# Channel products by seven block products, with weights and weight sums streamed from DRAM

## The chip, the cores and the metric

The kernel runs on one core of a Trainium2 chip. The metric is device time in microseconds of one execution; lower is better. Before the change three executions took 1118.13, 1116.75 and 1111.63 us, median 1116.75.

## The reference

Attention with a causal mask and a decay, then a token mixer and a channel mixer:

```python
batch, n_heads, seq, head_dim = (8, 8, 576, 64)      # B, H, S, D
scores = scale * q @ k.T                             # per head
decay = cum[:, None] - cum[None, :]                  # cum = cumsum(log f)
attn = softmax(where(causal, -1e9, scores + decay))
x = (attn @ v)                                       # (8, 576, 512)
xt = x.transpose(0, 2, 1)
h = np.maximum(xt @ w_tok1, 0.0) @ w_tok2            # tokens: 576 -> 256 -> 576
u = x + h.transpose(0, 2, 1)
h2 = np.maximum(u @ w_ch1, 0.0) @ w_ch2              # channels: 512 -> 1536 -> 512
return (u + h2).astype(np.float32)
```

B x S gives N = 4608 tokens. The channel mixer is the part that changes: per token two products with a 512 x 1536 and a 1536 x 512 matrix.

## The kernel before

**Precision.** A float32 product is made of three matmuls of a rounded type: each operand is split in a high part (ACT, `hi_act`, L575) and a low part, value minus high (`lo_dve` L584, on POOL `lo_pool` L581; behind a relu `lo_relu` L587), and high x high, low x high and high x low are summed in PSUM. So every product of a 128 x 128 weight block with up to 512 columns of tokens is three matmuls.

**Weights** come in as pairs of 32-bit words and are decoded by `decode` (L650): a raw tile `d_raw` of 128 x 512 pairs is loaded, some six steps on ACT and DVE (two tensor_scalars at L675 and L679, then L683, L687, L691) make float32 values in `d_g`, and ACT and DVE write their high and low parts. A piece of 512 columns is called a unit here.

**Stages.** First attention, head by head, with the token mixer of one batch entry laid between the heads of the next. `mixer` (L1193) transposes the attention output, makes the two token products (`tok1` L1252, `tok2` L1276) and, in the same pass, the first F1 = 2 of the NF = 12 hidden blocks of 128 of the channel mixer (`ch1` L1321, `ch2` L1349). It spills u (`ud`) and the partial channel sums (`pd`) to DRAM.

Then comes the channel stage with the remaining F2 = 10 hidden blocks, over nine chunks of 512 tokens. Its 20 weight units (10 of the first matrix, `w1r`, 10 of the second, `w2r`) stay in SBUF, in pools that `swap` (L1488) opens where attention's buffers were. `rest` (L743) decodes them; the first six run during the last mixer pass and the others early in the channel stage. `begin` (L1084) loads a chunk's u (into `xt`) and partial sums (into `part`), splits u into eight `ring` tiles and adds u to the partial sums on POOL. `up` (L1118) makes one hidden block: 12 matmuls of 512 columns (L1135 to L1137), relu and split (ACT L575, DVE L587) into `hid`. `down` (L1145) multiplies it into four PSUM accumulators by another 12 matmuls (L1156 to L1158); after the last block DVE adds the partial sums (L1169) and SP stores the result (L1173). The loop at L1177 runs `up` one block ahead of `down`.

**Order.** All instructions are registered with `Plan` (L362), a list scheduler that takes each with a priority, a cost and its buffers, and emits one fixed order per engine at build time. The priority counts blocks of the channel stage from `base`. SP issues all loads and stores in that order; a row that waits holds back what stands behind it.

Of the kernel before, what the change touches and what calls it, by code (L numbers as in the profile page):

```python
# [356 lines left out]

class Op:
# [3 lines left out]
class Plan:  # L362
# [9 lines left out]
    FIFO = ("ring", "xt", "part", "pr", "hl", "k1", "k2", "vv", "raw", "vr", "p34", "p2", "p1", "p0", "low", "hid", "d_raw", "d_g", "qf", "f34", "f2", "f1", "f0")  # L372
# [161 lines left out]
def build(nc, env, dims):  # L534
# [59 lines left out]
    cc = Buf("cc")  # L594

# [3 lines left out]
    def decay():  # L599
# [9 lines left out]
        p.op("POOL", 600, pr, lambda: nc.gpsimd.memset(row(2), 0.0), wr=["zero"], bufs=[w])  # L609
# [40 lines left out]
    def decode(prio, loads, w, hi, lo, tok, late=None):  # L650
        rb, gb = Buf("d_raw"), Buf("d_g")
# [6 lines left out]
        for i, (rows, cols, src) in enumerate(loads):  # L658
            dma(prio - 1.0, lambda a=(rows, cols, src): ld(*a), nb / len(loads), wr=[(rb, i)], bufs=[rb])
        rd = [(rb, i) for i in range(len(loads))]  # L660
# [38 lines left out]
        p.op("DVE", d_dve(w), prio, s6, port=True, rd=rd, wr=[gb], bufs=[rb, gb])  # L699
        p.op("ACT", d_act(w, False), prio, lambda: hi_act(hi(), asf(tl()[2])), rd=[gb, *([late] if late else [])], wr=[(tok, "h")], bufs=[gb])  # L700
# [3 lines left out]
        )  # L704

# [5 lines left out]
    def dec_list():  # L711
# [31 lines left out]
        def rest(i, which):  # L743
            def go(prio):
                if which == 1:
                    fs = sl((F1 + i) * P, P)
                    loads = [(full, sl(c * P, P), w_ch1[sl(c * P, P), fs]) for c in range(NC)]
                else:
                    loads = [(full, sl(0, C), w_ch2[sl((F1 + i) * P, P), :])]
                key = f"w{which}r"  # L750
# [5 lines left out]
            return go  # L756
# [3 lines left out]
        third = [rest(i, w) for i in range(F2) for w in (1, 2)]  # L760
# [296 lines left out]
    DB = PRM["DB"] if F1 else 0  # L1057
    whole = [(x * HS, HS, True) for x in range(2 * DB)]
    rest_, n_ch = N - DB * S, -(-(N - DB * S) // 512)
    cuts = [DB * S + x * rest_ // n_ch for x in range(n_ch + 1)]  # L1060
# [477 lines left out]
```

## Time and profile before

| what | before |
|---|---|
| three executions | 1111.63 to 1118.13 us, median 1116.75 |
| span of the profiled execution | 1116.7 us |
| granted TensorE clock in it, mean | 0.983 |
| PE busy | 1076.1 us |
| DVE, ACT, POOL busy | 633.4, 557.8, 536.7 us |
| moved by DMA | 148.43 MB |
| channel stage, first matmul start to last | 619.96 to 1111.82 us |

How to read the rows that follow below: PE is the matrix engine, PEld its weight loads, DVE, ACT and POOL the vector, scalar and general engines, SP the engine that issues DMAs. In a grouped row stand the source line, engine, operation, output <- inputs and a count, then busy time and mean nanoseconds of one, then idle time of the engine just before them and what ended it. In a timeline row the first number is the start and the second the duration; what stands in brackets is the idle time before it with its releaser. Durations overlap: two operations in a row can start closer together than one lasts, so the distance of starts, the pace, is what a busy engine spends on one.

### The profile page before, as it was taken

How to read it: one execution, taken by the hardware profiler on the slowest of the kernel's cores; microseconds unless marked ns; L12 is line 12 of the kernel's file. 1: busy time of each engine (PE TensorE's matmuls, PEld its weight loads, DVE VectorE, ACT ScalarE, POOL GpSimd, SP SyncE). 2: the span in 40 equal slices, each digit the busy share in tenths (PEclk: the TensorE clock that was granted, in tenths of full speed). 3: DMA queues.
4: the chain of work that ended last, by engine and by line, in shares of the span. 5: the costliest groups of instructions: out<-in, count | busy, mean ns of one | idle time of the engine just before them, and what ended most of it. 6: DMA issues, size and time to landing. Idle time of an engine off the chain costs nothing.

```text
span 1116.7 us, 18738 instructions
## 1 busy us (share of the span) xinstructions
PE 1076.1 (96%) x6442; PEld 939.2 (84%) x6442; DVE 633.4 (57%) x1618; ACT 557.8 (50%) x1441; POOL 536.7 (48%) x615
## 2 busy tenths in 40 slices
PE   8896988999999999999999999999999999999998
PEld 5565877899999999999998888888888888888886
DVE  5778989787887878888788992121212121111111
ACT  4675866788887888887885542111111111111110
POOL 4577797787868877787852205030312121111010
PEclk8898999999999999999999999999999999999999
DMA  8686587878768778687643635130303030302011
GB/s 198 157 202 149 153 214 179 209 197 201 208 168 209 201 193 218 168 214 192 168 132 131 183 102 175 36 114 1 113 1 113 1 113 0 114 19 57 24 53 38
DMA packets 70831, 148.43 MB, mean 133 GB/s; under 512 B 10008, under 2 KB 27416, under 8 KB 69712
## 3 DMA queue, kind: packets, MB, share of 16 engines
q1 hardware_dynamic: 70608, 147.22, 49.3%
q8 instruction: 51, 0.84, 0.3%
q14 instruction: 44, 0.36, 0.1%
q10 hardware_dynamic: 128, 0.01, 0.0%
HBM read 63.46 MB, written 28.31 MB: 82 GB/s over the span
## 4 chain that ended last, share of the span: by engine, by line
PE 77%; DVE 7%; DMA 7%; POOL 3%; ACT 2%; SPq 2%; issue 1%; DVEq 0%; POOLq 0%; ACTq 0%
PE bank L1135 7%; PE bank L1136 7%; PE bank L1137 7%; PE pair L1156 7%; PE pair L1158 7%; PE pair L1157 7%; PE bank L917 6%; DMA k<-hl 6%; PE bank L861 5%; PE pair L861 2%; PE pair L997 2%; PE pair L999 2%; PE bank L1276 1%; PE bank L1278 1%; PE pair L987 1%
## 5 line engine op out<-in xcount | busy, mean ns | idle before, releaser
L587 DVE SCALAR_TENSOR_TENSOR hid<-bank,hid 128x512 fp32r<-128x512 f32 x90 | 62.2, 691 | 337.1 <-ACT hid L575 336.9
L581 POOL TENSOR_TENSOR ring<-xt,ring 128x512 fp32r<-128x512 f32 (+1 forms) x68 | 92.3, 1372 | 315.4 <-ACT ring L575 314.6
L575 ACT ACTIVATE hid<-bank 128x512 fp32r<-128x512 f32 x90 | 53.8, 598 | 344.2 <-PE bank L1137 344.2
L903 POOL TENSOR_SCALAR pr<-pr,rec 128x576 f32<-128x576 f32 (+4 forms) x320 | 172.4, 558 | 38.4 <-DVE rec L896 31.0
L575 ACT ACTIVATE p<-bank 128x384 fp32r<-128x384 f32 (+2 forms) x300 | 128.5, 476 | 41.3 <-PE bank L917 38.9
L917 PE MATMUL bank<-ident,pr 128*128 128x128 f32 (+1 forms) x960 | 141.0, 282 | 7.9 <-DVE p L584 5.6
L1136 PE MATMUL bank<-ring,w1r 128*128 128x512 f32 x360 | 140.1, 389 | 0.0
L1135 PE MATMUL bank<-ring,w1r 128*128 128x512 f32 x360 | 140.1, 389 | 0.0
L1158 PE MATMUL pair<-hid,w2r 128*128 128x512 f32 x360 | 140.1, 389 | 0.0
L1157 PE MATMUL pair<-hid,w2r 128*128 128x512 f32 x360 | 140.1, 389 | 0.0
L1156 PE MATMUL pair<-hid,w2r 128*128 128x512 f32 x360 | 140.0, 389 | 0.0
L1137 PE MATMUL bank<-ring,w1r 128*128 128x512 f32 x360 | 140.0, 389 | 0.0
L875 ACT ACTIVATE pr<-bank,nmin 128x448 f32<-128x448 f32 (+3 forms) x256 | 118.3, 469 | 26.0 <-DVE nmin L868 23.8
L917 PEld LDWEIGHTS bank<-ident,pr 128*128 128x128 f32 (+1 forms) x960 | 110.6, 134 | 20.1 <-DVE p L584 6.1
L584 DVE TENSOR_TENSOR p<-bank,p 128x384 fp32r<-128x384 f32 (+1 forms) x180 | 106.1, 594 | 27.5 <-ACT p L575 26.4
L868 DVE CUSTOM_DVE_ANT_0 bank<-bank,mask 64x64 f32<-64x64 f32 (+3 forms) x256 | 106.7, 433 | 14.5 <-PE bank L861 12.7
L861 PE MATMUL bank<-k 128*128 128x320 f32 (+1 forms) x496 | 89.3, 301 | 9.4 <-DMA k<-hl 5.8
L861 PEld LDWEIGHTS bank<-k 128*128 128x128 f32 x496 | 75.6, 179 | 22.5 <-DMA k<-hl 5.5
L1158 PEld LDWEIGHTS pair<-hid,w2r 128*128 128x128 f32 x360 | 67.6, 188 | 14.2
L1137 PEld LDWEIGHTS bank<-ring,w1r 128*128 128x128 f32 x360 | 67.6, 188 | 14.1
L1156 PEld LDWEIGHTS pair<-hid,w2r 128*128 128x128 f32 x360 | 67.6, 188 | 14.0
L1136 PEld LDWEIGHTS bank<-ring,w1r 128*128 128x128 f32 x360 | 67.6, 188 | 14.0
(125 smaller groups left out, 2451.7 us busy)
## 6 DMA issues: line engine op xcount, KB each, us to landing
k<-hl SPq DMA_DIRECT2D x186, 288.0 KB
raw<-in_qk SPq DMA_DIRECT2D x31, 576.0 KB
vr<-in_v SPq DMA_DIRECT2D x32, 320.0 KB
ud<-xt SPq DMA_DIRECT2D x8, 1152.0 KB
pd<-part SPq DMA_DIRECT2D x32, 288.0 KB
out_t<-part SPq DMA_DIRECT2D x36, 256.0 KB
d_raw<-in_w_ch SPq DMA_DIRECT2D x12, 512.0 KB
d_raw<-in_w_ch SPq DMA_DIRECT2D x40, 128.0 KB
```

The source lines that it names most:

```text
L575: nc.scalar.activation(out, in_, func, scale=scale)
L861: nc.tensor.matmul(ps[:m, of : of + w], k[:, 0, i0 : i0 + m], k[:, 1, j0 : j0 + w], start=(x == 0), stop=(fq or x == 1))
L868: nc.vector.tensor_tensor_reduce(x, x, E["mask"][:m, a : a + w], -1.0 / D**0.5, 3e38, op0=ALU.add, op1=ALU.min, accum_out=E["nmin"][sm][:m ...
L875: nc.scalar.activation(at(pr)[:m, poff[t] : poff[t] + w], at(buf)[:m, of : of + w], AF.Exp, bias=E["nmin"][sm][:m, t : t + 1], scale=-1.0, ...
L903: nc.gpsimd.tensor_scalar(x, x, r, 0.0, op0=ALU.mult, op1=ALU.add)
L917: nc.tensor.transpose(out, at(pr)[:, poff[i] + start[j] : poff[i] + end[j]], E["ident"])
L1135: nc.tensor.matmul(q, wh[:, c, :], h_, start=(c == 0), stop=False)
L1136: nc.tensor.matmul(q, wl[:, c, :], h_, start=False, stop=False)
L1137: nc.tensor.matmul(q, wh[:, c, :], l_, start=False, stop=(c == NC - 1))
L1156: nc.tensor.matmul(q, wh, h_, start=(i == i0), stop=False)
L1157: nc.tensor.matmul(q, wl, h_, start=False, stop=False)
L1158: nc.tensor.matmul(q, wh, l_, start=False, stop=(i == NF - 1))
```

## The change

The channel stage is written anew. Three things change.

**768 tokens directly.** Two chunks, of 512 and 256 tokens (`PLAIN`), go through the ten hidden blocks as before, but block by block together: per block 12 matmuls of 512 and 12 of 256 up (`plain_up`, L1219 to L1221), and as many down (`plain_down`, L1239 to L1241). Meanwhile the weights are decoded. At the end DVE adds the partial sums (L1246) and SP stores (L1250).

**3840 tokens by seven products.** They form four super chunks of 2 x 480 tokens. Both channel products are done as a 2 x 2 block product by Strassen's scheme in Winograd's form, with seven block products in place of eight; the blocks are halves of the tokens and halves of the matrices. `prep` (L1301) makes the sums of u that the scheme needs and splits them. The up half goes over five pairs q of hidden blocks: per pair seven `uprod` of 6 matmuls with 480 columns (L1365 to L1367), the results combined from PSUM by ACT and DVE into four float tiles `H` (`plus` L1287, and L1390, L1396, L1402). The down half goes over the seven products: `product` (L1409) splits an operand made of `H` tiles into a `st` or `hid` tile for each pair and multiplies it (`mul`, 6 matmuls, L1440 to L1442); `diff` (L1277) makes the next operands out of the `H` tiles on DVE; `join` and `leave` (L1472, L1480) combine the results with partial sums and u, which `rest_in` (L1450) loads and POOL adds, and store them. So a super has 5 x 7 x 6 matmuls up and as many down. The first 42 up matmuls of the next super are laid between the last 42 down ones of this one.

**Weights through DRAM.** `unit` (L721) takes the place of `rest`. A unit is now four blocks of 128 x 128. Beside the split that it had (`pw` tile), DVE makes four sums of its blocks (128 columns each), these are split too (`sg` tile), and both are stored to DRAM (`wd`), 393 KB and 524 KB. In the supers one 256 KB tile of them is loaded per product (`weights`, L1296) into twelve half tiles. In exchange SBUF no longer holds all the weights; the raw, ring and token weight tiles are used again for other purposes, and a third `swap` opens `H` and `st` tiles after the direct stage.

The core of the diff:

```diff
-        def rest(i, which):
-                decode(
-                    prio, loads, C, lambda: E[key][i][:, 0, :], lambda: E[key][i][:, 1, :], (key, i),
-                    late=f"gate{int(i >= PAIRS0)}",
-                )
+    def unit(prio, loads, which, q, k, gate_, i):
+        gb = decode(prio, loads, C, None, None, i, late=gate_)
+        pb, sb = Buf("pw"), Buf("sg" if i < 8 else "sg2")
...
+        for out, a, b, op in ((0, (0, 3), (0, 2), ALU.add), (1, (1, 0), (0, 0), ALU.subtract), (3, (0, 1), (1, 1), ALU.subtract), (2, (0, 0), (0, 3), ALU.subtract)):
+            p.op(
+                "DVE", d_dve(P), prio + SLAG / UNIT,
+                lambda out=out, a=a, b=b, op=op: nc.vector.tensor_tensor(blk(1, out), blk(*a), blk(*b), op=op),
...
+        for x, (b, z0, z1) in enumerate(((pb, 0, 3), (sb, 3, 7))):
+            dma(
+                prio, lambda b=b, z0=z0, z1=z1: nc.sync.dma_start(E["w_d"][which][q][:, z0:z1, k], asf(at(b)[:, : z1 - z0])), P * 1024 * (z1 - z0), rate=340,
...
-    base = HB + 20
+    base = HB + 220
...
+    for i in range(F2):
+        clock = i * tile_us
+        for ch in chunks:
+            plain_up(i, ch)
+        if i:
+            clock = (i - 1) * tile_us
+            for ch in chunks:
+                plain_down(i - 1, ch)
...
+    def weights(which, q, z):
+        wq = Buf("wq")
+        dma(
+            pr(14), lambda: nc.sync.dma_start(asf(at(wq)), E["w_d"][which][q][:, z]), P * 2048,
...
+        def uprod(q, z, bank, first, fin, extra=(), more=()):
+            wq = weights(1, q, z)
+            bs = [ub[z, k] for k in (0, 1)]
...
+                for k in (0, 1):
+                    wt, h_, l_ = at(wq)[:, k], at(bs[k][0])[:, :w], at(bs[k][1])[:, :w]
+                    nc.tensor.matmul(o, wt[:, 0, :], h_, start=(first and k == 0), stop=False, skip_group_check=True)
+                    nc.tensor.matmul(o, wt[:, 1, :], h_, start=False, stop=False, skip_group_check=True)
+                    nc.tensor.matmul(o, wt[:, 0, :], l_, start=False, stop=(fin and k == 1), skip_group_check=True)
...
+        def product(z, src, bank, first, relu, fin=False, lead=9.0):
...
+            for x in range(FX):
+                st, hb = Buf("st"), H[x][src]
...
+                dve(
+                    lead, lambda st=st, hb=hb: (lo_relu if relu else lo_dve)(at(st)[:, 1, :w], at(hb)[:, :w], at(st)[:, 0, :w]),
...
+        product(0, 0, "a", True, False, lead=25.0)
...
+        for x in range(FX):
+            diff(b12[x], b12[x], b11[x], 18.0 - 1.3 * x, True)
+        product(3, 1, "c", True, False)
...
+        product(2, 2, "d", False, False, fin=last)
+        leave(1, 0, "d", 2 if last else 1)
```

Everything up to the last mixer pass keeps its order on every engine. Three places of the order differ in ways that matter below.

The first is DVE in that last mixer pass (the batch entry's `ring` tiles are the hidden tokens of the token product, which PE waits for; `d_g`, `tmp` are weights in decoding). Before:

```order
L584 TENSOR_TENSOR ring_138<-bank_67,ring_135 128x512
L584 TENSOR_TENSOR ring_140<-bank_65,ring_139 128x512
L584 TENSOR_TENSOR ring_141<-bank_68,ring_141 64x256
L1290 TENSOR_TENSOR xt_130<-bank_66,xt_130 128x288
L1290 TENSOR_TENSOR xt_130<-bank_67,xt_130 128x288
L584 TENSOR_TENSOR w1r_6911<-d_g_146,w1r_6911 128x512
L675 TENSOR_SCALAR d_g_147<-d_g_147 128x512
L587 SCALAR_TENSOR_TENSOR ring_137<-bank_65,ring_136 128x512
```

After:

```order
L593 TENSOR_TENSOR ring_149<-bank_67,ring_149 64x256
L593 TENSOR_TENSOR pw_6918<-d_g_156,pw_6918 128x4x128
L690 TENSOR_SCALAR d_g_157<-d_g_157 128x512
L686 TENSOR_SCALAR tmp_6921<-tmp_6921 128x512
L694 SCALAR_TENSOR_TENSOR d_g_157<-d_raw_155,d_g_157 128x512
L690 TENSOR_SCALAR tmp_7244<-tmp_6921 128x512
L698 TENSOR_TENSOR d_g_157<-d_g_157 128x512
L694 SCALAR_TENSOR_TENSOR tmp_7244<-d_raw_154,tmp_7244 128x512
L702 SCALAR_TENSOR_TENSOR d_g_157<-d_raw_155,d_g_157 128x512
L596 SCALAR_TENSOR_TENSOR ring_151<-bank_65,ring_150 128x512
```

Ahead of the relu of the hidden tokens (the last row of each) now stand steps of two units in decoding.

The second is SP where the supers begin. Before, in the channel stage, it only fetched chunks and stored results:

```order
L1093 DMA xt_130<-ud_110 128x4x320
L1173 DMA out_t<-part_151 128x512
L1173 DMA out_t<-part_150 128x512
L1096 DMA part_151<-pd_116 128x128
L1096 DMA part_151<-pd_117 128x384
```

After:

```order
L1250 DMA out_t<-d_raw_153 128x256 x2
L1250 DMA out_t<-d_raw_154 128x256
L1296 DMA pw_6915<-wd_1_124 128x512
L1250 DMA out_t<-d_raw_154 128x256
L1296 DMA pw_6915<-wd_1_124 128x512
L1296 DMA pw_6916<-wd_1_124 128x512
L1296 DMA pw_6918<-wd_1_124 128x512
L1296 DMA pw_6916<-wd_1_124 128x512
L1296 DMA pw_6918<-wd_1_124 128x512
L1458 DMA d_raw_153<-pd_116 128x384
```

Weight tiles of the supers (`pw<-wd`) now stand between and behind the stores of the direct tokens, and the loads of partial sums and u behind them.

The third is DVE in the channel stage. Before, one relu a block and four adds a chunk:

```order
L587 SCALAR_TENSOR_TENSOR hid_6913<-bank_65,hid_6913 128x512
L1169 TENSOR_TENSOR part_148<-pair_63,part_148 128x512
L587 SCALAR_TENSOR_TENSOR hid_6913<-bank_66,hid_6913 128x512
L1169 TENSOR_TENSOR part_150<-pair_63,part_150 128x512
L1169 TENSOR_TENSOR part_149<-pair_64,part_149 128x512
```

After, in the down half of a super:

```order
L1402 TENSOR_TENSOR h_8389<-bank_65,tmp_8393 128x480
L1334 TENSOR_TENSOR xt_140<-xt_140 128x480
L593 TENSOR_TENSOR hid_6922<-h_8376,hid_6922 128x480
L593 TENSOR_TENSOR hid_6923<-h_8380,hid_6923 128x480
L1281 SCALAR_TENSOR_TENSOR h_8376<-h_8375,h_8376 128x480
L1281 SCALAR_TENSOR_TENSOR h_8380<-h_8379,h_8380 128x480
L593 TENSOR_TENSOR hid_6924<-h_8384,hid_6924 128x480
L593 TENSOR_TENSOR w2l<-xt_140,w2h 128x480
```

Low parts of operands (L593), differences of `H` tiles (L1281) and sums of the next super's u (L1334) alternate, where relus stood alone.

More of the change, by code (lines that the diff above doesn't have):

```diff
@@ L371 @@
     START = dict(PE=3000, DVE=900, ACT=1900, POOL=1810, SP=700)
-    FIFO = ("ring", "xt", "part", "pr", "hl", "k1", "k2", "vv", "raw", "vr", "p34", "p2", "p1", "p0", "low", "hid", "d_raw", "d_g", "qf", "f34", "f2", "f1", "f0")
+    FIFO = ("ring", "xt", "part", "pr", "hl", "k1", "k2", "vv", "raw", "vr", "p34", "p2", "p1", "p0", "low", "hid", "hidB", "pw", "sg", "sg2", "uh", "uh2", "H", "st", "wq", "q", "rr", "g2", "d_raw", "d_g", "qf", "f34", "f2", "f1", "f0")
     def __init__(self):
@@ L650, in decode @@
     def decode(prio, loads, w, hi, lo, tok, late=None):
-        rb, gb = Buf("d_raw"), Buf("d_g")
+        rb, gb = Buf("d_raw"), Buf("g2" if late and tok > 1 else "d_g")
         nb = P * w * 8
@@ new lines, in build, with pr, weight, tile_of @@
+    FX = F2 // 2
+    W = (N - sum(PLAIN)) // 8
+    clock = 0.0
+    def pr(lead=0.0):
+        return base + (clock - lead) / UNIT
+    def weight(which, i, c):
+        k, m = (c, i % 2) if which == 1 else (i % 2, c)
+        unit_ = pw[which, i // 2, (c % 2)]
+        half, row = (c // 2, i % 2) if which == 1 else (i % 2, c // 2)
+        return unit_, (0, 3, 1, 2)[2 * half + row]
+    def tile_of(which, i, c):
+        b, x = weight(which, i, c)
+        return at(b)[:, x, 0, :], at(b)[:, x, 1, :]
@@ new lines, in build, with dve, diff, f @@
+    gate("gate2", [q for q in p.ops if any(z.kind in ("pw", "g2") for z in q.bufs)], lambda: E["swap"](2))
+    w = W
+    mm1 = w / 2.4e3 + 0.013
+    clock = tile_us * F2
+    NSC = (N - T1) // (2 * w)
+    last = False
+    def dve(lead, fn, **k):
+        return p.op("DVE", d_dve(w), pr(lead), fn, **k)
+    def diff(out, a, b, lead, relu=False):
+        def f():
+            o_, a_, b_ = (at(x)[0][:, at(x)[1], :w] if isinstance(at(x), tuple) else at(x)[:, :w] for x in (out, a, b))
+            if relu:
+                nc.vector.scalar_tensor_tensor(o_, a_, 0.0, b_, op0=ALU.max, op1=ALU.subtract)
+            else:
+                nc.vector.tensor_tensor(o_, a_, b_, op=ALU.subtract)
+        dve(lead, f, rd=[a, b], wr=[out], bufs=list({a, b, out}), port=True)
@@ L1444, in attn_mixer_kernel @@
     E["part_d"] = [dram.tile([P, NC, S], F32, name=f"pd{b}") for b in range(B)]
+    E["w_d"] = {which: [dram.tile([P, 7, 2, 2, P], F32, name=f"wd{which}_{q}") for q in range(F2 // 2)] for which in (1, 2)}
+    E["q"] = E["acc"] | E["one"]
+    E["two"] = E["accB"] = E["one"]
+    E["sg"], E["uh"] = {}, {}
+    for nm in ("t1h", "t1l", "t2h", "t2l", "w1h", "w1l", "w2h", "w2l"):
+        x = E[nm].rearrange("p a b -> p (a b)")
+        if nm[:2] == "t1":
+            E["sg"][((nm, 0), (nm, 1))] = x[:, : 2 * C].rearrange("p (z h n) -> p z h n", z=4, h=2)
+        for i in (0, 1):
+            E["uh"][((nm, i),)] = x[:, i * C : (i + 1) * C]
+    E["sg2"], E["uh2"] = E["sg"], E["uh"]
     for _ in range(3):
```

533 lines of the change are left out of this document (415 added, 118 removed).

## The prediction

> **What bounds the kernel now.** I read the page's totals first, then the forty slices, the chain, and last the windows and single rows of the channel stage, where the change lies.
>
> ```profile
> PE 1076.1 (96%) x6442; PEld 939.2 (84%) x6442; DVE 633.4 (57%) x1618; ACT 557.8 (50%) x1441; POOL 536.7 (48%) x615
> PE   8896988999999999999999999999999999999998
> DVE  5778989787887878888788992121212121111111
> PE 77%; DVE 7%; DMA 7%; POOL 3%; ACT 2%; SPq 2%; issue 1%; DVEq 0%; POOLq 0%; ACTq 0%
> L587 DVE SCALAR_TENSOR_TENSOR hid<-bank,hid 128x512 fp32r<-128x512 f32 x90 | 62.2, 691 | 337.1 <-ACT hid L575 336.9
> L1158 PEld LDWEIGHTS pair<-hid,w2r 128*128 128x128 f32 x360 | 67.6, 188 | 14.2
> ```
>
> PE is busy 96% of 1116.7 us. The slices show two regimes: up to about slice 23 DVE is nearly as full as PE; from there, the channel stage, DVE falls to 1 or 2 tenths while PE stays at 9. The only DVE work there, 90 relus, idles 337 us waiting on ACT, which waits on PE. So in this stage the matmul count times the period of one matmul is the time, and DVE and DMA are nearly free. The windows say how free (columns: us, then busy time and count of PE, weight loads, DVE, ACT, POOL, then clock, DMA share, GB/s):
>
> ```profile
> 0.00:560.00 560.00, 525.89 (x3822) 475.65 (x3823) 454.25 (x1305) 427.04 (x1192) 423.04 (x518) 0.97 0.75 190
> 620.00:640.00 20.00, 20.00 (x90) 16.53 (x90) 19.67 (x35) 9.24 (x16) 1.29 (x1) 1.00 0.61 193
> 641.00:642.00 1.00, 1.00 (x7) 0.80 (x6) 0.97 (x3) 0.73 (x2) 0.00 (x0) 1.00 0.80 256
> 649.00:650.00 1.00, 1.00 (x6) 0.83 (x5) 1.00 (x4) 0.20 (x1) 0.00 (x0) 1.00 0.88 263
> 685.00:687.00 2.00, 2.00 (x10) 1.68 (x9) 0.28 (x1) 0.00 (x0) 0.60 (x1) 1.00 1.04 322
> 688.00:690.00 2.00, 2.00 (x11) 1.65 (x10) 0.57 (x1) 0.93 (x2) 0.21 (x1) 1.00 1.06 377
> 700.00:800.00 100.00, 100.00 (x443) 82.81 (x442) 17.73 (x27) 15.16 (x26) 20.49 (x16) 1.00 0.19 57
> ```
>
> From 700 to 800 us PE is busy throughout at full clock, DVE 18%, DMA 57 GB/s.
>
> **Part 1, the matmuls.** Periods come from starts on PE's timeline.
>
> ```profile
> 619.96 0.40 PE L1135 MATMUL bank<-ring,w1r 128*128 128x512 f32 x1
> 1101.16 0.39 PE L1156 MATMUL pair<-hid,w2r 128*128 128x512 f32 x1
> 1106.60 0.39 PE L1156 MATMUL pair<-hid,w2r 128*128 128x512 f32 x1
> 601.28 0.28 PE L1252 MATMUL bank<-ring,t1h 128*128 128x256 f32 x1
> 604.51 0.28 PE L1253 MATMUL bank<-ring,t1l 128*128 128x256 f32 x1
> 606.71 0.29 PE L1276 MATMUL bank<-t2h,ring 128*128 128x288 f32 x1
> 608.31 0.29 PE L1276 MATMUL bank<-t2h,ring 128*128 128x288 f32 x1
> 1111.82 0.39 PE L1158 MATMUL pair<-hid,w2r 128*128 128x512 f32 x1
> ```
>
> The two starts 5.44 us apart in the second and third row are 24 matmuls (one block up, one down): 0.2267 us each at 512 columns. The 256-column pair is 27 intervals in 3.23 us: 0.1196. The difference is 0.000418 us a column, and 288 columns come to 0.133 by it: 12 intervals in 1.60 us agree. So 480 columns should take 0.2133. Before: 9 chunks x 10 blocks x 24 = 2160 matmuls of 512, 489.7 us (619.96 to 1111.82 is 491.9, of which 2.4 are the last 18 matmuls of the mixer's second channel product, which only move ahead of the stage in the new order: no net cost). After: 240 of 512 (54.4) and 240 of 256 (28.7) direct, then 4 supers x (210 up + 210 down) = 1680 of 480 (358.3): 441.4. The term is 441.4 - 489.7 = **-48.3 us**. It is a gain only if everything that the seven products need keeps up with a PE that is already full; the other parts price that.
>
> **Part 2, DVE ahead of the direct stage.** DVE's durations and paces:
>
> ```profile
> 631.90 0.42 DVE L675 TENSOR_SCALAR d_g<-d_g 128x512 uint32<-128x512 uint32 x1
> 632.23 0.68 DVE L587 SCALAR_TENSOR_TENSOR hid<-bank,hid 128x512 fp32r<-128x512 f32 x1
> 632.84 0.68 DVE L584 TENSOR_TENSOR w2r<-d_g,w2r 128x512 fp32r<-128x512 f32 x1
> 633.43 0.42 DVE L679 TENSOR_SCALAR d_g<-d_g 128x512 uint32<-128x512 uint32 x1
> 633.89 0.69 DVE L683 SCALAR_TENSOR_TENSOR d_g<-d_raw,d_g 128x512 f32<-128x512 uint32 x1
> 586.33 0.55 DVE L584 TENSOR_TENSOR p<-bank,p 128x384 fp32r<-128x384 f32 x1
> 587.86 0.20 DVE L584 TENSOR_TENSOR low<-bank,p 64x64 fp32r<-64x64 f32 x1
> 605.46 0.69 DVE L587 SCALAR_TENSOR_TENSOR ring<-bank,ring 128x512 fp32r<-128x512 f32 x1 [2.29 <-ACT ring L575]
> 606.21 0.40 PE L1276 MATMUL bank<-t2h,ring 128*128 128x288 f32 x1 [1.41 <-DVE ring L587]
> ```
>
> Start to start, a 512-column op takes 0.605 us and a tensor_scalar 0.335 (0.455 where it needs the op just ahead of it, 633.43 to 633.89). 0.55 against 0.68 for 384 and 512 columns is 0.0011 a column, so 480 columns are 0.571 and 128 about 0.20. In the last mixer pass PE waits 1.41 us on one DVE relu, and DVE had idled 2.29 just before it. In the new order DVE has six 512-column ops, four tensor_scalars and one 128-column op more in that stretch (weights are decoded two and three units at a time): 3.6 + 1.3 + 0.2 = 5.2 us. What idled and what ran slow there, 2.8 us, absorbs the rest: **+2.4**, between 0 (if DVE takes these after the relu in effect, by running ahead) and +5.2.
>
> **Part 3, the direct stage.** One block now lasts 12 x 2 x (0.2267 + 0.1196) = 8.31 us of PE, and two weight units are decoded in it. From block 3 to block 9 DVE has 9 decodes, 10 sets of four 128-column sums with their low parts, 13 relus and 5 ops of 480: 50.5 us by the paces above, against 6 x 8.31 = 49.9 of PE. With all 18 tensor_scalars at the dependent price it is 52.7: **+2.8**. That is a dead heat, as the window 620 to 640 (DVE 19.67 of 20) shows DVE can be: bounds 0 and +12.7 (each op at its duration, 0.69, not at its pace). DMA: a unit loads 0.52 MB and stores 0.92 MB, 1.44 MB in about 5.5 us = 262 GB/s; the loads of the same raw weights in 1 KB runs reach 256 to 263 GB/s at shares of 0.80 to 0.88, about 305 at a full share. It fits, with little to spare; the stores stand on the same queue, SP's, ahead of the next raw loads, so a late low part holds back the loads behind it, and the three raw buffers are what hides that.
>
> **Part 4, into the supers.** The first super's splits of u and the second hidden pair's weights come late: on SP those weights stand behind the stores of the direct tokens, which wait for their adds. The first six products have their buffers filled ahead, 1.28 us of PE each. I take **+1.5**, between 0 and +4 (three products late).
>
> **Part 5, the supers.** A super is 420 x 0.2133 = 89.6 us of PE. DVE has about 120 ops of 480, 68.4 us, so on average it is covered; it was 18 us in 100. But the ops are not even: a hidden pair of the up half has 7 or 8 (4.0 to 4.6 us in 8.96), the down half 84 (48.0 us in 44.8), since each product's operand is built, rounded high and low per pair. The next super's first 42 up matmuls are laid between the last 42 down ones, so the down half lasts nearer 52. Six operand buffers let DVE run six steps (7.7 us) ahead. I take +1 a super, **+4** in all, bounds 0 and +40. POOL adds eight sums a super beside it, all due in the light half; what POOL does to DVE:
>
> ```profile
> 610.34 1.56 DVE L691 SCALAR_TENSOR_TENSOR d_g<-d_raw,d_g 128x512 uint32<-128x512 uint32 x1
> 611.82 1.93 DVE L687 TENSOR_TENSOR d_g<-d_g 128x512 f32<-128x512 f32 x1
> ```
>
> Beside POOL two such ops took 1.56 and 1.93 us, not 0.69: about 1 us lost each, 8 us a super, inside the 21 us that DVE has free; without that cover they would cost it in full.
>
> DMA in a super: 70 tiles of 256 KB of weights (18.4 MB), u twice, partial sums and the output (7.9 MB): 26.2 MB in 89.6 us = 292 GB/s, five times what the stage moves now. The rows 685 to 690 (u and partial sums in 2 KB runs) reach 322 and 377 at a share of 1.04 to 1.06. The new tiles have 2 KB runs too. SP takes its instructions in order, so the weights also stand behind stores that wait for DVE's adds; twelve tiles, 15 us of products, hide that. I take no wait from it, and keep the other end for rival C. How such loads are issued:
>
> ```profile
> 685.75 4.72 SPq L1096 DMA_DIRECT2D part<-pd  x6
> 1110.95 2.65 DVE L1169 TENSOR_TENSOR part<-pair,part 128x512 f32<-128x512 f32 x4 [2.83 <-PE pair L1158]
> 1111.67 2.29 SPq L1173 DMA_DIRECT2D out_t<-part  x4
> ```
>
> SP spends 4.72 / 6 = 0.79 us on an issue; some 90 issues a super are 71 us of 89.6. The Trainium skill, "DMA: Bandwidth & Descriptors", section "Anatomy of one DMA", gives about 2.0 us fixed plus bytes at 436 GB/s for one transfer (measured on GpSimd's path), and its "Bandwidth" section asks for 1 MiB or more; an estimate by it is 2.6 us for a 256 KB tile, 182 us a super if they came one after another, and so speaks against this change. The trace does not agree with "one after another": 322 GB/s over 2 us is 2.5 tiles landed in 2 us, so several overlap. By the page the sum would end near 1450; loading in that fashion is the far end of rival C.
>
> **Part 6, the end.** The last matmul starts at 1111.82 and the span ends at 1116.7, with four adds of 512 and four stores behind it. The new end adds two halves of 240 columns, two stores: **-0.8** (0 to -1.5).
>
> **The sum**, against the profiled execution, whose span of 1116.7 is also the median of the three runs (1116.75): 1116.7 - 48.3 + 2.4 + 2.8 + 1.5 + 4.0 - 0.8 = **1078.3 us**. Call it case A. Its own range is 1066 to 1092: the lower end has every addition at nothing (1066.8), the upper the direct stage and the supers some 7 each beyond what I took.
>
> **Rivals.**
>
> B, DVE sets the pace of the down halves. If its 480-column ops cost their duration (0.55 + 96 x 0.0011 = 0.66) and not their pace, 84 are 55.4 us against 44.8 of PE. Half the operand buffers' lead (3.8) pays for some: 6.8 a super, 27 in place of 4: 1101. For it: DVE at 19.67 of 20 us in the decode window shows no reserve to draw on, and every operand passes ACT first. Against: there 512-column ops held their pace of 0.605.
>
> C, the other side: the weight stream sets the pace of the supers. Loads and stores mixed ran, over the first 560 us, 190 GB/s at a share of 0.75: 253 at a full share. At that rate a super's 26.2 MB take 103.6 us, 14.0 over PE, 56 for four in place of 4: 1130. It decides from 261 GB/s downward: there a super takes 100.2 us, and the 42.4 us of four such delays eat the gain. Fewer than three tiles in flight would do the same: the stores at the end need about 3 us each (the last is issued near 1113.5, the end is 1116.7), so two in flight give 175 GB/s, three 262. Against: 256 KB transfers in 2 KB runs reached 322 and 377, and the program has twelve tiles to fill.
>
> D, the matmuls don't get shorter: a 480-column matmul keeps 0.2267, because the weight load ahead of it (188 ns, the row above) and its switch set the period. 1680 x 0.0134 = 22.5: 1100.8. Against: 288 and 256 columns scale, at 0.133 and 0.1196, with the same weight loads.
>
> **How the numbers follow.** A has a chance of 0.70, B 0.14, C 0.10, D 0.06. The forecast is A's 1078.3. The range reaches from 1065 to 1103, so that it takes in B's and D's times; outside are C and the outer parts of the others, about 0.2. One per cent, 11.2 us, is about what can be told from no change here. Faster than 1105.6 are A, B, D and a fifth of C: 0.92. Within 1%: 0.03, from C near its break-even; slower than 1127.9: 0.05, the other half of C.
>
> **What would show it.** Right: the matmul starts of the supers 0.2133 apart, PE busy 9 tenths or more throughout, DMA near 290 GB/s in the supers and DVE near 0.75; direct stage 83 to 90 us, a super 89.6 to 92. B would show as PE idle before L1440 released by DVE on st or hid tiles, C as PE idle before L1365 or L1440 released by DMA on pw tiles, D as a 0.227 period. The prediction is wrong if supers take over 96 us, or if the time before the direct stage grows by more than 5.

## The result and the profile after

The changed kernel takes 1087.28 us (median of four runs, 1086.0 to 1093.99), the kernel before 1116.05 (median of four as well). The ratio is 0.9759, interval 0.9725 to 0.9794: faster by 2.4%. The forecast was 1078.3 us, with a range of 1065 to 1103. The profiled execution took 1088.3 us with a span of 1086.1, 30.6 less than the 1116.7 that the prediction started from.

The page of the changed kernel: totals, the slices of PE, DVE and DMA, and the chain.

```profile
PE 1037.6 (96%) x6442; PEld 921.1 (85%) x6442; DVE 887.8 (82%) x2114; ACT 646.9 (60%) x1607; POOL 496.6 (46%) x579
PE   8897888999999999999999899999999999999998
DVE  5778989787787888878879999975995896797486
DMA  8686577686877868777675799789999889979874
PE 69%; DVE 11%; DMA 9%; POOL 4%; SPq 3%; issue 2%; ACT 2%; DVEq 0%; POOLq 0%; ACTq 0%
```

PE is as full as before, 96%, with 38.5 us less to do. What was nearly free behind it is not any more: in the last sixteen slices DVE goes from 1 or 2 tenths to between 4 and 9, DMA from mostly 0 to 3 to between 7 and 9 (4 in the very last). The stages, as windows (the direct stage, the first two supers, the last one; columns as in the prediction):

```profile
625.90:710.90 85.00, 84.07 (x482) 73.59 (x481) 84.03 (x196) 40.19 (x76) 0.00 (x0) 1.00 0.93 302
710.90:808.10 97.20, 93.54 (x423) 78.03 (x422) 78.00 (x129) 37.43 (x66) 23.60 (x14) 1.00 0.93 308
808.10:899.60 91.50, 91.47 (x421) 78.53 (x420) 73.62 (x122) 34.74 (x61) 11.62 (x9) 1.00 0.90 289
990.90:1082.20 91.30, 91.24 (x421) 78.43 (x419) 61.00 (x100) 27.32 (x46) 6.91 (x6) 1.00 0.73 231
```

From the second super on PE does not stop. The first one has 3.7 us of idle PE in it and takes 6 us more than the others. The starts that measure the terms, from PE's timeline:

```profile
577.44 0.30 PE L1576 MATMUL bank<-ident,xt 128*128 128x128 f32 x1
586.95 0.55 PE L956 MATMUL bank<-ident,pr 128*128 128x128 f32 x3 [0.26 <-POOL pr L942]
588.55 1.09 PE L956 MATMUL bank<-ident,pr 128*128 128x128 f32 x8 [1.05 <-POOL pr L942]
602.01 1.20 PE L1576 MATMUL bank<-ident,xt 128*128 128x128 f32 x9 [1.35 <-DVE xt L1083]
604.10 0.39 PE L1609 MATMUL bank<-ring,t1h 128*128 128x256 f32 x1 [0.88 <-DVE ring L593]
609.88 0.40 PE L1633 MATMUL bank<-t2h,ring 128*128 128x288 f32 x1 [2.19 <-DVE ring L596]
625.90 0.39 PE L1219 MATMUL bank<-ring,pw 128*128 128x512 f32 x1
710.92 0.38 PE L1365 MATMUL bank<-w1h,pw 128*128 128x480 f32 x1
798.99 0.38 PE L1365 MATMUL bank<-w1h,pw 128*128 128x480 f32 x1
808.09 0.38 PE L1365 MATMUL bank<-t2h,pw 128*128 128x480 f32 x1
1082.00 0.38 PE L1442 MATMUL pair<-hid,pw 128*128 128x480 f32 x1
```

Between 798.99 and 808.09 lie 42 matmuls without a stall: 0.2167 us each, not the 0.2133 that 512 and 256 columns led to. In the last mixer pass PE waits three times for DVE, and twice for POOL (at 586.95 and 588.55), 5.7 us in all; in the same pass of the kernel before it waits 0.50 us for ACT and 1.41 for the relu, 1.9 in all. The pass begins with transposes (the row at 577.44). In the kernel before they began at 577.90:

```profile
577.90 0.31 PE L1219 MATMUL bank<-ident,xt 128*128 128x128 f32 x1
```

Set against the steps of the prediction, in us:

| term | predicted | measured | how |
|---|---|---|---|
| fewer and shorter matmuls | -48.3 | -42.6 | 1680 x 0.2167 = 364.0 in place of 358.3 |
| ahead of the direct stage | +2.4 | +3.5 | the pass is 4.0 longer beyond the 2.4 of moved matmuls, and began 0.5 earlier |
| direct stage | +2.8 | +1.9 | 85.0 - 83.1 |
| into and through the supers | +5.5 | +7.3 | 1082.00 + 0.2 - 710.92 = 371.3, less 364.0 |
| end | -0.8 | -0.8 | last start to end of span: 4.1, was 4.9 |
| sum | -38.4 | -30.7 | span: -30.6 |

### The profile page after: what moved, and what is told of

The parts are those of the page before. It is cut to its first block, busy times and chain, and to the rows that moved or that the text cites. A ratio compares the mean times of both kernels' runs of the same rounds, so it can differ in the third digit from the quotient of the medians.

```text
span 1086.1 us, 20523 instructions
## 1 busy us (share of the span) xinstructions
PE 1037.6 (96%) x6442; PEld 921.1 (85%) x6442; DVE 887.8 (82%) x2114; ACT 646.9 (60%) x1607; POOL 496.6 (46%) x579
## 4 chain that ended last, share of the span: by engine, by line
PE 69%; DVE 11%; DMA 9%; POOL 4%; SPq 3%; issue 2%; ACT 2%; DVEq 0%; POOLq 0%; ACTq 0%
PE bank L956 7%; DMA k<-hl 6%; PE bank L900 5%; PE bank L1365 5%; PE bank L1367 5%; PE bank L1366 5%; PE bank L1441 3%; PE bank L1440 3%; PE bank L1442 3%; PE pair L1440 3%; PE pair L1441 3%; PE pair L1442 2%; PE pair L900 2%; PE pair L1036 2%; PE pair L1038 2%
## 5 line engine op out<-in xcount | busy, mean ns | idle before, releaser
L942 POOL TENSOR_SCALAR pr<-pr,rec 128x576 f32<-128x576 f32 (+4 forms) x320 | 174.1, 563 | 40.4 <-DVE rec L935 35.2
L593 DVE TENSOR_TENSOR p<-bank,p 128x384 fp32r<-128x384 f32 (+1 forms) x180 | 106.0, 594 | 27.8 <-ACT p L584 26.8
L826 POOL TENSOR_TENSOR hl<-raw,hl 128x1152 fp32r<-128x1152 f32 x28 | 74.7, 2667 | 1.4
L584 ACT ACTIVATE hid<-h 128x480 fp32r<-128x480 f32 x77 | 46.6, 606 | 47.9 <-PE bank L1441 26.9
L1038 PE MATMUL pair<-p,vv 128*128 128x512 f32 x240 | 74.4, 318 | 0.0
L1036 PE MATMUL pair<-p,vv 128*64 128x512 f32 x240 | 71.5, 339 | 0.0
L587 POOL TENSOR_SCALAR p<-low 64x576 fp32r<-64x576 f32 x60 | 42.4, 707 | 60.3 <-DVE low L593 53.2
L584 ACT ACTIVATE ring<-bank 128x288 fp32r<-128x288 f32 (+2 forms) x96 | 46.6, 497 | 18.7 <-PE bank L1576 7.4
L826 POOL TENSOR_TENSOR vv<-vr,vv 128x640 fp32r<-128x640 f32 x30 | 47.8, 1594 | 19.5 <-ACT vv L816 19.3
L593 DVE TENSOR_TENSOR low<-bank,p 64x64 fp32r<-64x64 f32 (+1 forms) x120 | 50.8, 441 | 6.9 <-ACT p L584 6.3
L907 DVE CUSTOM_DVE_ANT_0 pair<-pair,mask 128x576 f32<-128x576 f32 x64 | 48.8, 763 | 7.1 <-PE pair L900 7.0
L590 POOL TENSOR_TENSOR ring<-xt,ring 128x576 fp32r<-128x576 f32 x32 | 45.1, 1420 | 17.2 <-ACT ring L584 16.5
```

Source lines behind the costliest of these rows:

```text
L584: nc.scalar.activation(out, in_, func, scale=scale)
L593: nc.vector.tensor_tensor(out, in_, asf(hi), op=ALU.subtract)
L826: (nc.gpsimd if eng == "POOL" else nc.vector).tensor_tensor(out, in_, asf(hi), op=ALU.subtract)
L907: nc.vector.tensor_tensor_reduce(x, x, E["mask"][:m, a : a + w], -1.0 / D**0.5, 3e38, op0=ALU.add, op1=ALU.min, accum_out=E["nmin"][sm][:m ...
L942: nc.gpsimd.tensor_scalar(x, x, r, 0.0, op0=ALU.mult, op1=ALU.add)
L1036: nc.tensor.matmul(x[:D], at(vv)[:, v0 + j, :D], at(pb)[:, 1, c0 : c0 + w], start=False, stop=last)
```

## Experiments

### Is 0.2167 us the price of the width?

```diff
+        for i in range(count // 6):
+            b = banks[n % 8]
+            n += 1
+            for j in range(6):
+                nc.tensor.matmul(b[:, :n_], w[:, (0, 1, 0, 2, 3, 2)[j], :], x[:, (0, 0, off)[j % 3] : (0, 0, off)[j % 3] + n_], start=(j == 0), stop=(j == 5))
```

> Only matmuls: groups of 120 with 512, 496, 480, 480 (low operand at column 480), 464, 448, 416, 384, 320, 288, 256, 512 and 480 columns, six to a PSUM bank and a new weight block for each, no DMA, DVE or ACT work beside them; the whole computation of the reference is left out. In the changed kernel's supers the starts of 480-column matmuls are 0.2167 us apart, not the 0.2133 of the prediction. If the width alone sets that, 480 columns stand at 0.2167 here too, and other widths show from where a matmul costs more than its columns. If the supers' traffic (DMA at 290 GB/s, DVE) stretches it, 480 columns stand at 0.2133 here.

The kernel holds matmuls alone, in groups of one width. From the timeline, stretches of one width each (start, time from the first start to the last end, count), and from the groups the mean duration of one:

```profile
10.69 3.56 PE L41 MATMUL bank<-x,w 128*128 128x512 f32 x15
43.68 3.68 PE L41 MATMUL bank<-x,w 128*128 128x496 f32 x16
64.71 3.63 PE L41 MATMUL bank<-x,w 128*128 128x480 f32 x16
121.80 3.52 PE L41 MATMUL bank<-x,w 128*128 128x464 f32 x16
139.74 3.61 PE L41 MATMUL bank<-x,w 128*128 128x448 f32 x17
```

```profile
L41 PE MATMUL bank<-x,w 128*128 128x480 f32 x360 | 78.3, 378 | 0.0
L41 PE MATMUL bank<-x,w 128*128 128x512 f32 x240 | 56.4, 397 | 4.0 <-ACT w L27 4.0
```

For 480 columns (3.63 - 0.378) / 15 = 0.2168 us, wherever the low operand lies. The same working gives 0.226 for 512, 0.220 for 496, 0.210 for 464, 0.203 for 448, and 0.187, 0.173, 0.147, 0.132 and 0.120 for 416, 384, 320, 288 and 256. On the line through 256 and 512, 480 should have cost 0.213. So the width alone sets it: 448 to 480 columns stand about 3 ns above the line, 496 and 416 on it. Traffic has no part in it: the 480 columns cost here, with no DMA beside them, what they cost in the middle supers at 287 to 289 GB/s. And contrary to its expectation this kernel does have some DMA, eight stores in its first 30 us: the 512-column stretch at 10.69 ran beside them at 419 GB/s and kept the 0.226 that a later stretch shows without DMA. Why 448 to 480 columns stand above the line is not known. The Trainium skill, "TensorE: Matmul & The Clock Gate", section "Back-to-back issue gap", gives columns / 2.4 + 2.5 ns for one warm matmul alone; by that an estimate for 480 columns is 0.2025 us, and the trace, a stream with a weight load for each matmul, doesn't agree.

### Does PE set the pace of the supers?

Sixty matmuls more in each:

```diff
-                for k in (0, 1):
+                for k in (0, 1) * (1 + (z == 0)):
...
-                    for j in js:
+                    for j in js * (1 + (z == 0)):
```

> In every super the matmuls of the first of the seven products are issued twice (60 more, as many as an eighth product has), same order, DMA, DVE and ACT; the sums are wrong by that. Theory (PE sets the pace of the supers): each super is 60 x 0.2167 = 13.0 us longer, 52 us in all, 1139 us: more than the kernel before, the gain is the product saved and nothing else. Rival (DVE or DMA already set the pace in the supers): the added matmuls fill PE's idle time and cost less than 45 us.

1140.49 us, one run. The timeline of this kernel, where its second and third super begin (480 matmuls apart):

```profile
821.93 0.38 PE L1440 MATMUL pair<-st,pw 128*128 128x480 f32 x1
926.16 0.38 PE L1365 MATMUL bank<-ring,pw 128*128 128x480 f32 x1
```

104.2 us are 480 x 0.2172. Every added matmul costs its full period, as the theory had it: from the second super on PE alone sets the pace. It also says what the saved product is worth. With as many matmuls as eight products have, and all else that the change brings, the kernel is slower than before (1117 in that comparison).

### How near are the other bounds?

A third of the matmuls less:

```diff
                     nc.tensor.matmul(o, wt[:, 0, :], h_, start=(first and k == 0), stop=False, skip_group_check=True)
-                    nc.tensor.matmul(o, wt[:, 1, :], h_, start=False, stop=False, skip_group_check=True)
                     nc.tensor.matmul(o, wt[:, 0, :], l_, start=False, stop=(fin and k == 1), skip_group_check=True)
```

(and the same in `mul`.) What the edit leaves out is the low weights by the high operand, not, as the expectation says, the high weights by the low operand; the number of matmuls is the same.

> In the supers every third matmul (high weights by low operand) is left out, so PE has 60.7 us of work a super in place of 91; DVE, ACT, DMA and the order stay. This measures how far off the other engines' bounds are. Theory (DMA is next: 26.2 MB a super at the 340 GB/s that full slices reach): 77 us a super, whole kernel 1030 to 1045 us, PE idle on pw tiles behind DMA. Rival (DVE is next, by the down half): near 70 us a super, PE idle behind DVE on st tiles, about 1010 us. If neither binds: 61 us a super, 965 us.

1061.06 us, one run, later than either theory had it. The supers take 94.8, 86.9, 89.9 and 72.5 us: 30 us of PE are gone and in the first three 1 to 5 us are saved. PE's waits over the supers (total, times, longest), and one window of an up half and one of a down half:

```profile
PE bank L1365 <- DMA pw<-wd: 27.4, 19, 3.7
PE bank L1440 <- DVE hid L596: 8.1, 4, 3.4
```

```profile
831.00:851.00 20.00, 16.69 (x60) 12.65 (x60) 11.13 (x19) 6.43 (x12) 2.83 (x2) 0.80 1.04 367
871.00:891.00 20.00, 17.33 (x75) 14.22 (x74) 20.00 (x36) 9.93 (x19) 1.22 (x1) 0.95 0.80 251
```

In the up half DMA is at its end (share 1.04, 367 GB/s) while DVE has room; in the down half DVE works 20.00 of 20 us while DMA has room. Neither of the two expected bounds holds alone: they take turns, and the buffers between don't even it out. The changed kernel itself shows the same in the same two windows, with PE never idle in them:

```profile
831.00:851.00 20.00, 20.00 (x93) 17.05 (x92) 12.46 (x21) 5.56 (x10) 2.49 (x3) 1.00 1.00 344
871.00:891.00 20.00, 20.00 (x94) 17.29 (x94) 19.01 (x34) 11.57 (x20) 0.64 (x1) 1.00 0.80 237
```

DMA is at its end in the first, DVE nearly so in the second. That both are near is the finding. With a third of the matmuls gone, the second and third super still take 87 to 90 us, though DVE's mean load is only 74 of 91: what the prediction took as 21 us of cover is far less. How much less this run doesn't settle, since the granted clock fell in it as well (0.80 and 0.95 in the windows), so that PE's work shrank by less than a third and part of the 87 to 90 us is PE's own.

### What does the first super lose?

Half of the weight bytes:

```diff
-            pr(14), lambda: nc.sync.dma_start(asf(at(wq)), E["w_d"][which][q][:, z]), P * 2048,
+            pr(14), lambda: nc.sync.dma_start(asf(at(wq)[:, 0]), E["w_d"][which][q][:, z, 0]), P * 2048,
```

(and both halves of the products read the first half of the tile.)

> Of each 256 KB weight tile of the supers only the first half is loaded, and used for both halves of the product: 9.2 MB less DMA a super, the same instructions otherwise. The first super takes 97.2 us, the others 91.2. Theory (the first super's 6 us are weight tiles that come late): the first super falls to 92 to 93, the others stay at 91.1: 1082 to 1083 us. Rival (it is DVE, late with the splits of u and the adds of the direct tokens): the first super stays above 95, the time within 2 us of the changed kernel's.

1087.06 us, and the windows of its first two supers:

```profile
715.30:811.90 96.60, 93.11 (x423) 78.22 (x422) 77.50 (x131) 37.48 (x66) 18.52 (x14) 1.00 0.69 215
811.90:903.10 91.20, 91.20 (x421) 78.64 (x420) 72.64 (x122) 34.78 (x61) 11.23 (x9) 1.00 0.64 190
```

With 215 GB/s in place of 308 the first super is 0.6 us shorter. My theory fell: the bytes of the weights aren't what it loses. PE's waits in the first super (total, times, longest) say more; first the two largest of the changed kernel, then the largest of this one:

```profile
PE bank L1365 <- DMA pw<-wd: 1.9, 2, 1.0
PE bank L1365 <- DVE h L1402: 0.8, 1, 0.8
```

```profile
PE bank L1440 <- DVE h L1396: 1.2, 1, 1.2
```

The changed kernel waits 1.9 us for weight tiles there and 1.7 for DVE and ACT; with half the bytes the first are gone and the second have grown to 3.5. Behind one wait stood the other. The rival, DVE, was tested next by taking work from it in the direct stage:

```diff
-        for out, a, b, op in ((0, (0, 3), (0, 2), ALU.add), (1, (1, 0), (0, 0), ALU.subtract), (3, (0, 1), (1, 1), ALU.subtract), (2, (0, 0), (0, 3), ALU.subtract)):
-            p.op(
-                "DVE", d_dve(P), prio + SLAG / UNIT,
...
-        o = p.op("DVE", d_dve(C), prio + SLAG / UNIT, lambda: lo_dve(at(sb)[:, :, 1, :], blk(1), at(sb)[:, :, 0, :]), rd=[*every, (sb, 0)], wr=[(sb, 1)], bufs=[gb, sb], port=True)
...
+        o = p.op("ACT", d_act(C, False), prio + SLAG / UNIT, lambda: hi_act(at(sb)[:, :, 1, :], blk(0)), rd=[gb, (sb, 0)], wr=[(sb, 1)], bufs=[gb, sb])
```

> The four 128-column weight sums per unit and their low part are left out on DVE (the stored sum tiles hold the unit's own blocks, written by ACT), so the products use wrong sums; some 80 small and 20 wide DVE ops less (20 x (0.8 + 0.605) = 28 us of DVE), the same DMA and matmuls. Theory (after the run with half of the weights: the first super's 6 us and the 1.9 of the direct stage are DVE work that a full direct stage pushes on): the first super falls from 97 to 92 or 93, the direct stage to 83.3, together 5 to 6 us, 1081 us. Rival (SP's loads and weights late): the first super stays at 96 to 97, within 2 us of the changed kernel.

The first super starts and ends here at

```profile
712.50 0.38 PE L1358 MATMUL bank<-w1h,pw 128*128 128x480 f32 x1
804.87 0.37 PE L1433 MATMUL pair<-st,pw 128*128 128x480 f32 x1
```

92.4 us, and the direct stage takes 84.4: 5.4 us less, as expected of DVE. The whole is 1085.18, not 1081. The third super takes 92.6 in place of 91.2, and the last mixer pass, up to the second token product, 35.1 us (575.51 to 610.63) in place of 32.4. That pass in this kernel and, below it, in the changed one:

```profile
575.51:610.63 35.12, 28.49 (x205) 26.59 (x203) 28.69 (x56) 25.28 (x57) 10.43 (x9) 0.95 0.60 196
577.44:609.88 32.44, 26.72 (x205) 25.02 (x203) 30.41 (x67) 21.00 (x48) 9.58 (x9) 1.00 0.53 175
```

DVE has less to do there, but ACT 4.3 us more, since the edit lets ACT write the low part as well; and of the 2.7 us 1.8 are PE being busy longer, at a granted clock of 0.95. So the run takes work from DVE and gives some to ACT, and its gain in the first super is the sum of both.

The loads of the direct tokens are a second part. First merged, then left out:

```diff
-                    base + (9 if y else -1), lambda of=of, b=b, s=s, w=w, c=c, cv=cv: nc.sync.dma_start(cv(c)[:, of : of + w], E["part_d"][b][:, c, s : s + w]),
...
+                                lambda of=of, b=b, s=s, w=w, c=c, bx=bx, nm=nm, cw=cw: nc.sync.dma_start(
+                                    at(bx)[:, : 2 * cw].rearrange("p (a n) -> p a n", a=2)[:, :, of : of + w], E[nm][b][:, c : c + 2, s : s + w]
+                                ),
```

> The 16 loads of partial sums and u of the 256 direct tokens, which stand on SP ahead of the first super's weights (705.97 to 714.1 us), become 8 of twice the size: same bytes, 8 issues of 0.47 us less. Theory (SP's issues hold the weights back): weights start 3 to 4 us earlier, the first super loses 1 to 3 us less. Rival (bytes, not issues, hold them back; or DVE): no difference over 0.5 us.

1085.65 us. The first super takes 94.8 (711.04 to 805.87), 2.4 less, as the theory had it. But the third takes 93.3 in place of 91.2: PE waits 1.57 us there for a weight tile. The four supers together take 371.0, as much as the changed kernel's 371.3.

```diff
-        for c in range(NC):
+        for c in range(NC) if not y else ():
...
+                    (lambda c=c: nc.vector.tensor_scalar(cv(c), av_(c), 1.0, 0.0, op0=ALU.mult, op1=ALU.add)) if y else (lambda c=c: nc.vector.tensor_tensor(cv(c), av_(c), cv(c), op=ALU.add)),
```

> From the changed kernel the partial sums and u of the 256 direct tokens are left out: 16 loads on SP, four POOL adds; DVE only copies the sums from PSUM to the output tiles (so these tokens miss their partial sums and u). Theory (the first super's loss has two parts: DVE's late splits, some 3.5 us, and the direct tokens' adds that wait for these loads, some 2.5): first super 94 to 95 us. Rival A (only DVE's backlog counts): 96 to 97. Rival B (these loads are all of it): 92 or less.

```profile
710.32 0.38 PE L1366 MATMUL bank<-w1h,pw 128*128 128x480 f32 x1
804.98 0.37 PE L1366 MATMUL bank<-ring,pw 128*128 128x480 f32 x1
```

94.7 us for the first super (1085.83 for the kernel): between the rivals, where the theory put it. So of its 6 us, 2.5 hang on the loads of partial sums and u for the 256 tokens, issued from 706 to 714 us with DVE's last adds behind them. Merging these loads had gained as much as leaving them out, with the same bytes and the same adds: that points at the time that SP spends on issues, though each edit also gives the kernel an order of its own. For the rest DVE's backlog is the likely cause. The two shares can't simply be added: 4.8 us went with the sums on DVE and 2.5 with the loads, together 7.3 of 6.2, so the same time waits on both. Each is read from one profile.

### What does the last mixer pass lose?

```diff
-        p.op("DVE", d_dve(w, True) * (m2 if late else 1.8), prio, s2, wr=[gb], bufs=[gb], port=True)
+        p.op("DVE", d_dve(w, True) * (m2 if late else 1.8), prio, s2, rd=[("hidden", B - 1)] if late and tok > 3 else [], wr=[gb], bufs=[gb], port=True)
...
```

> In the last mixer pass the decode steps of units from the fifth on wait for the relu of the hidden tokens, so that DVE does that relu without them ahead of it. Theory (the 3.5 us by which the direct stage starts late are DVE's decode steps, and DVE is full from there to the supers): the direct stage starts 2 to 3 us earlier, but the direct stage or the first super take as much longer: total within 1.5 us. Rival (DVE has room later): 2 to 3 us faster.

1091.57 us. Its ratio to the kernel before, 0.9776 (0.9753 to 0.98), overlaps that of the changed kernel, so the whole times alone don't tell the two apart; in the profiles the way from the transposes of the last mixer pass to the last matmul takes 510.4 us here and 504.6 in the changed kernel. The pass shortens only from 32.4 to 31.5 us, and the first super takes 103.9, with PE waiting up to 2.76 us for weights and 1.88 for splits. Held from the third unit on (`tok > 1`):

> As the run that held the decode steps, but from the third unit on, so that DVE has no decode step of them ahead of the last relu of the hidden tokens. In the changed kernel the stretch of the last mixer pass from the transposes that start at 577.44 us to the first matmul of the second token product (609.88) takes 32.4 us; in the kernel before it takes 28.3 (577.90 to 606.21); with decode held from the fifth unit it took 31.5. Theory (all of the 4.1 us are decode steps ahead of several DVE operations of that pass, not of the relu alone): 28 to 29.5 us here, paid back with more in the direct stage and the first super, total 1092 to 1105 us. Rival (the order of PE or ACT in that pass makes it, and decode only the 0.9 us seen): 31 us or more.

1101.49 us, one run. From the transposes to the second token product it is

```profile
574.69 0.31 PE L1576 MATMUL bank<-ident,xt 128*128 128x128 f32 x1
605.10 0.40 PE L1633 MATMUL bank<-t2h,ring 128*128 128x288 f32 x1 [1.41 <-DVE ring L596]
```

30.4 us, between the two theories: 2.0 of the 4.1 us are decode steps from the third unit on. Of the other 2.1 the rows name a part: PE waits 3.3 us in this pass, 1.4 more than before the change, and these are 0.38 for the `xt` sum (L1083) ahead of the transposes at 597.56 and 1.05 for their split (L593) behind them. In the kernel before, twelve matmuls of the second token product stand between these transposes and the next product (599.32 to 601.28); in the new order of PE the product follows at once. No run changed that order, so this part is read and not shown, and the rest stays open. The waits for POOL are gone here too: its scaling of the last head (L942) took 3.59 us, in the changed kernel, beside more decode on DVE, 4.81. The price of the 2.0 is plain: the direct stage takes 91.7 us (85.0) and the first super 103.5 (97.2), and from the transposes to the last matmul it is 520.8 us, not 504.6. Decode ahead of the stage pays for its waits many times over.

### Can POOL take some of it?

POOL stands idle in the direct stage. This kernel has the merged loads and the earlier weights of the next one, and the adds of the first chunk on POOL:

```diff
-            eng = "POOL" if y else "DVE"
+            eng = "POOL"
...
```

> The kernel with merged loads and earlier weights (first super 94.6 us there), and the four 512-column adds of u to the partial sums of the first direct chunk moved from DVE to POOL, which stands idle there for 95 us: 4 x 0.605 = 2.4 us of DVE less in the full direct stage. Theory (DVE work pushed on is what the first super loses): first super 93 us or less, direct stage shorter by up to 1 us, 1083 to 1084 us. Rival (POOL's adds slow the DVE ops beside them by as much as they save, as 1.46 in place of 0.66 us in the first super shows): no difference over 0.5 us.

1087.29 us; the first super takes 99.0, not 93. Three of POOL's four adds (the second row holds two) and DVE beside them, from both timelines of this kernel:

```profile
629.78 1.88 POOL L1205 TENSOR_TENSOR part<-part,xt 128x512 f32<-128x512 f32 x1 [17.45 <-DMA d_raw<-in_w_ch]
637.87 3.05 POOL L1205 TENSOR_TENSOR part<-part,xt 128x512 f32<-128x512 f32 x2 [4.36 <-DMA part<-pd]
```

```profile
629.83 0.69 DVE L698 TENSOR_TENSOR tmp<-tmp,tmp 128x512 f32<-128x512 f32 x1
630.43 0.69 DVE L596 SCALAR_TENSOR_TENSOR hid<-bank,hid 128x512 fp32r<-128x512 f32 x1
631.03 1.17 DVE L702 SCALAR_TENSOR_TENSOR tmp<-d_raw,tmp 128x512 uint32<-128x512 uint32 x1
638.10 1.67 DVE L694 SCALAR_TENSOR_TENSOR d_g<-d_raw,d_g 128x512 f32<-128x512 uint32 x1
639.69 1.38 DVE L735 TENSOR_TENSOR tmp<-tmp,tmp 128x128 f32<-128x128 f32 x1
```

Some DVE ops with two SBUF inputs stretch, from 0.69 to 1.17 and 1.67 us, a 128-column one from the 0.29 that such sums take there otherwise to 1.38; the sum at 629.83 has two as well and kept its 0.69, and so did the relu that reads PSUM (630.43). Four adds save 2.4 us of DVE; these stretches alone take 2.6 back. So the rival's mechanism is seen, but not its size: the first super is 4.4 us longer than in the kernel below, not the same. The rest of that loss wasn't taken apart. The Trainium skill, "GPSIMD Engine Reference", section "1. Specifications", says that GpSimd shares its SBUF interfaces with VectorE, with contention for instructions that have two SBUF inputs; the three stretched rows agree, the one at 629.83 shows none.

### A better version?

```diff
-            pr(14), lambda: nc.sync.dma_start(asf(at(wq)), E["w_d"][which][q][:, z]), P * 2048,
+            pr(20), lambda: nc.sync.dma_start(asf(at(wq)), E["w_d"][which][q][:, z]), P * 2048,
```

> Merged loads as in the run of that name, and all weight tiles of the supers registered 6 us earlier, so that more of them stand on SP ahead of the direct tokens' stores and of the loads of partial sums. Theory: the waits on pw tiles that were left (1.1 us in the first super, 1.6 in the third) go, 1083 to 1084 us. Rival (the twelve buffers limit the lead, and later stores or loads of u come late instead): no gain over the merged loads, 1085 to 1088 us.

1085.58 us; the supers take 94.6, 91.9, 91.2 and 91.3. Again, in five rounds:

> The kernel with merged loads and weights registered earlier once more, in five rounds: 1085.58 us before, against 1087.28 of the changed kernel. From the last DMA wait of attention to the last matmul it took 534.3 us, the changed kernel 536.8. If that holds, 1084 to 1086 us; if it was chance, 1087 or more.

1084.64 us, ratio 0.9714 (0.9691 to 0.9738) to the kernel before; the supers take 95.2, 91.8, 91.6 and 91.4. It beats the kernel before. Against the changed kernel the intervals overlap, and from the transposes of the last mixer pass to the last matmul it took 502.1 us in one run and 504.3 in the other, the changed kernel 504.6. So 0 to 2.5 us are gained, not settled which.

## Why the prediction was right, and where it was off

The forecast lay 7.8 us of span below what came (-38.4 for -30.6).

**What bounds it.** Right: the channel stage was matmul count times period, and still is from the second super on. The run with an eighth product's matmuls shows it, each at its full 0.217 us.

**The matmul term** is the one that was mis-sized most: -42.6 for -48.3. The 256- and 512-column periods were right (0.120 and 0.226 in the kernel of matmuls alone), but the line between them does not hold at 480. Rival D had asked whether the period would shrink at all; it shrank by three quarters of what was taken. The 3.4 ns make 5.7 of the 7.8 us. The trace of before held a hint at most: where two matmuls of 448 columns follow each other in attention (as at 421.73 and 421.94 us), their starts are 0.20 to 0.21 us apart in most pairs, and the line gives 0.200; no longer series of a width between 384 and 512 stands in it.

**Ahead of the direct stage** +3.5 for +2.4, inside the bounds. The working priced one wait, for the relu. PE waited five times: for three operations of DVE (L1083 by 1.35 us, L593 by 0.88, the relu by 2.19) and twice for POOL (1.31). Decode steps stand ahead of L1083 and of the relu; ahead of L593 DVE itself idled 1.39 us for ACT's split of the transposes, which had come late. About half of the pass's loss was shown to be decode; the rest is read from rows or open.

**The direct stage**, +1.9 for +2.8: right, a dead heat, DVE busy 84.03 of 85.00 us.

**The transition and the supers**, +7.3 for +5.5, but placed wrongly. The +1 for each super did not come: the last three lose 0.5 us each at most. The first one loses 6.2. That the two sum near the forecast is chance: 2.9 us of the +4 that didn't come paid for more than half of the 4.7 by which the transition was underpriced. The first super's cause lies where the transition step looked, at four times the price: DVE enters the first super with the work that the full direct stage pushed on (without the sums on DVE 4.8 us were gone), and the stores and loads of the direct tokens stand in between (2.5, overlapping). Of the weights behind them on SP, the other half of that step, the bytes matter little: halving them moved 0.6 us, since waits for DVE took the place of the waits for weights.

**DMA and DVE as bounds (C and B).** Neither came, as forecast, at 287 to 289 GB/s and DVE 74 of 91 us in the middle supers. But the margin was misjudged: with a third of the matmuls left out the first three supers stayed at 87 to 95 us. The margin is well below the 21 us of free DVE time that the working gave, since DVE and DMA are each full in one half of a super; the fallen clock of that run keeps it from a figure.

**The end**, -0.8: right.

**Its own signs.** Two of them went against it. The first super took 97.2 us, over the 96 that it had named as a sign of being wrong, and the matmul starts of the supers were 0.2167 apart, not 0.2133. The direct stage began 5.9 us later than the stage before, but 2.4 of these are the matmuls that moved. PE busy 9 tenths or more and DMA near 290 GB/s came as said; DVE was at 0.80 in the second super, not 0.75.

## What to carry to other kernels

When a bound engine's work is cut, price the engines behind it half-stage by half-stage: two resources that are free on average can each be full in turn, and the next cut may then gain little. A full stage pushes its debt into the next one, so look for the loss at the first stretch behind it. Measure the period of an instruction at the very size that the change uses; it need not lie on the line between two known sizes.

## What the runs showed of the hardware

- Matmuls of three-product form with a weight load each: 0.2267 us at 512 columns start to start, 0.220 at 496, 0.2167 at 480, 0.210 at 464, 0.203 at 448, 0.187 at 416. 480 columns cost nearly as much as 496. DMA at 419 GB/s beside 512-column matmuls left their 0.226 as it was.
- Beside POOL's adds some DVE operations with two SBUF inputs took 0.5 to 1.1 us longer each (the rows at 631.03, 638.10 and 639.69), another (629.83) did not, and one that reads PSUM (630.43) did not.
- In the run with a third of the matmuls left out, where PE's waits reached 3.7 us, the granted clock was 0.80 and 0.95 in the two 20 us windows; in the supers of the changed kernel, where none is over 1.01 us, it is 1.00. In the run that held the decode steps from the fifth unit on, a stretch with PE busy 1.52 of 3.40 us was followed by one at a clock of 0.50:

```profile
707.50:710.90 3.40, 1.52 (x8) 1.00 (x7) 3.40 (x8) 1.34 (x3) 0.00 (x0) 1.00 1.06 399
711.10:714.30 3.20, 3.20 (x9) 2.22 (x9) 3.20 (x7) 1.75 (x4) 0.00 (x0) 0.50 1.05 394
```
